# A norm, squares and additions redistributed over GpSimd, TensorE and ScalarE in a fused convolution, adaLN and expert kernel

## The chip, the cores and the metric

One core of one Trainium2 chip runs the whole program. A time is the device time of one execution in microseconds (us), the smaller the better. A run more than 1.5% above the fastest of its kernel counts as slow and is left out of the ratios. A ratio is the mean time of one kernel's fast runs over that of the kernel before's fast runs in the same rounds on the same chip, so it isn't quite the ratio of the medians that stand beside it.

## The reference, cut to what matters

```python
x = A_q                                        # 2048 tokens x 640 channels
sa, ca, ga, sb, cb, gb = (silu(c) @ w_mod)     # six rows of 640
h = layernorm(x) * (1 + ca) + sa               # the first norm
kv = shift_conv(A_k) * A_v                     # 4 taps
y  = irfft(rfft(pad(kv)) * rfft(pad(ssm_k)))[:2048] + kv * ssm_D
x  = x + ga * (h * y)                          # h is needed only here
h2 = layernorm(x) * (1 + cb) + sb              # the second norm
r  = h2 @ w_r ; idx = top8(r)
x  = x + gb * (h2 + scatter(idx, sigmoid(r[idx]) * expert(h2[idx])))
```

The kernel does the long convolution as Fourier transforms by matmul, for five blocks of 128 channels one after the other: transform, a complex product on VectorE, inverse transform, a round trip of the output U through DRAM, a last small transform, and `x += h * y`. After block 4 come the second norm, the choice of the eight tokens, and the expert.

## The kernel before: the parts that the argument touches

The order of the whole program is a list of tokens; each advances one generator by a step. `H` makes h in four groups of four token rows, three steps to a group; `P` is the complex product; `BT` the inverse transform; `AT` the last transform and the update of xq; `GB`, new in the changed kernel, the two gate products. The other tokens are other stages.

```python
def t_H():
    h = h_["h"] = big.tile([P, M, D], BF, name="h", tag="h")
    for m4 in range(4):
        for m in range(4 * m4, 4 * m4 + 4):
            V.tensor_scalar(out=h[:, m, :], in0=xq[:, m, :], scalar1=rs1[:, m:m + 1], scalar2=nm1[:, m:m + 1], ...)
        hq = h[:, 4 * m4:4 * m4 + 4, :]
        yield
        V.tensor_tensor(out=hq, in0=hq, in1=og[:, None, :].to_broadcast([P, 4, D]), op=ALU.mult)
        yield
        V.tensor_tensor(out=hq, in0=hq, in1=sg[:, None, :].to_broadcast([P, 4, D]), op=ALU.add)
        yield

def t_P(b):
    for hk in range(2):
        # ... cut
        V.tensor_tensor(out=T2[:], in0=X, in1=Hi, op=ALU.mult)          # 128 x 2048
        V.tensor_tensor(out=X, in0=X, in1=Hr, op=ALU.mult)
        yield
        V.tensor_tensor(out=Xr, in0=Xr, in1=T2[:, :, 1, :], op=ALU.subtract)   # 128 x 1024
        V.tensor_tensor(out=Xi, in0=Xi, in1=T2[:, :, 0, :], op=ALU.add)
        yield
```

The squares for the second norm are 23 ScalarE activations with an accumulator and nine statistics instructions on VectorE; the root of the first norm is a chain of small VectorE instructions. In the order, all of `H` stands between blocks 2 and 3, ahead of block 2's last store of U.

Of the kernel before, what the change touches and what calls it, by code (L numbers as in the profile page):

```python
# [35 lines left out]
LK0 START TC RA DIAG0 RA TAB0 RAT LG0 LK1 C0:2 TAB0 G0 LG1 TAB1:2 G0*:2 LX G0* DIAG1 C1:2 DIAG2 BG0 LXA0 BG0*  # L36
IT* Sx RAT G1 BG0 G1:3 DIAG3 Sx:2 IT*:2 X0 X0* BG1 LXA1 X0 X0* BG1 LX:2 LW BG1:2 LK2 Sx:4 X1 BX0 BX0*:2 BX0
P0:2 X1:3 BG0 LG2 LW LK3 C2:2 MOD Sx DIAG4 Sx LX LW Sx:2 P0:2 G2:3 BT0 BX1 LXA2 C3 G2 BX1 BT0 Sx:2 BT0 BX1 MOD
LW MOD LW P1 BX1 X2:3 Sx:4 LG3 C3 X2 BT0 MOD LW LXA3 P1:2 LK4 BG2:2 BX2 LG4 P1 BX2:3 BG2:2 MOD:2 OG BT1 P2:4
G3 X3:2 BT1 COL G3:2 H:3 G3 G4:2 C4 BT1 H BT1 H X3:2 C4 LXA4 LU0 G4:2 BG3 BX3:2 H:3 BT2 H:4 BX3 BG3:3 BT2:3 P3  # L40
AT0 P3 LU1 X4:4 AT0 BX3 BG4 P3:2 BX4:3 BG4 AT1 WG BT3 LU2 BT3:3 BG4:2 P4:2 AT1 BX4 R0 BT4:2 P4:2 R0 AT2:2
BT4:2 LU3 AT3 R1 AT3 R1 R2* BS*:2 R2 R3* LU4 AT4:2 BS* S:3 R3 R4* SV R4 S SA:2 WD BS:3 T BS:2 BL N:5 N* T N*
WG N* N:2 T N N* N:3 N* F T F:3 BL F T:2 F:3 T:4
# [17 lines left out]
def _kernel_body(ctx, tc, A_q, A_k, A_v, A_shift_k, A_ssm_k, A_ssm_D,  # L61
# [5 lines left out]

    def dump(name, ap):
        if name in DBG:
            nc.sync.dma_start(out=DBG[name], in_=ap)  # L70
# [6 lines left out]
    psum = ctx.enter_context(tc.tile_pool(name="psum", bufs=4, space=bass.MemoryType.PSUM))  # L77

    def ps_tile(shape, dtype=F32):
        return psum.tile(list(shape), dtype, name="ps", tag="ps")  # L80
# [42 lines left out]
    bias = const.tile([P, 4], F32, name="bias")  # L123
# [25 lines left out]
    cinfo = const.tile([P, 3], BF, name="cinfo")  # L149
    bcol = const.tile([NB * NSEL, 1], F32, name="bcol")  # L150
    gb40 = const.tile([NB * NSEL, P], BF, name="gb40")
# [8 lines left out]
    def t_START():  # L160
# [4 lines left out]
        G = nc.gpsimd  # L165
        for i, v in enumerate((PI, -PI, -math.pi / 2, -4096.0)):
            G.memset(bias[:, i:i + 1], v)
        nc.scalar.activation(out=junk1[:], in_=bias[:, 2:3], func=ACT.Sin)
        iota(pint[:], [[0, 1]], cm=1)
        iota(a4.rearrange("p (a e) -> p a e", e=8), [[4, M], [0, 8]], base=1)  # L170
        iota(pidx[:], [[0, 1]], cm=1)
        make_identity(nc, ident[:])
        iota(erow[:], [[0, M], [1, 8]])
# [4 lines left out]
        for hf in range(2):  # L178
            iota(trig[:, hf, :].rearrange("p (a b) -> p a b", a=8), [[4, 8], [64, P]], base=32 * hf + 1)
            if hf == 0:  # L180
                G.memset(Dt[:], 0.0)
        iota(arow[:], [[1, M], [0, 8]])
        iota(irow[:], [[1, P]])
        G.memset(onesb[:], 1.0)
# [4 lines left out]
        V.tensor_scalar(out=mint[:], in0=pint[:], scalar1=15, scalar2=None, op0=ALU.bitwise_and)  # L189
        V.tensor_copy(out=mcol[:], in_=mint[:])  # L190
        yield

    def t_TC():
# [9 lines left out]
        G.tensor_scalar(out=bcol[:], in0=bcol[:], scalar1=-MAGIC, scalar2=None, op0=ALU.add)  # L203
        G.tensor_scalar(out=cinfo[:, 0:1], in0=mC[:], scalar1=128.0, scalar2=None, op0=ALU.mult)
# [60 lines left out]
    As, HXs, Uds, uAs, diags = {}, {}, {}, {}, {}  # L265
# [21 lines left out]
    def t_C(b):  # L287
        kT, vT = kTs[b], vTs[b]
        kvT = ring.tile([P, S_TOK], BF, name="kvT", tag="V")
        for i2 in range(2):  # L290
            ps = ps_tile([P, 2, 512])
            for i in range(2):
                n0 = 16 + 512 * (2 * i2 + i)
                for j in range(4):
                    nc.tensor.matmul(ps[:, i, :], lhsT=diags[b][:, j, :], rhs=kT[:, n0 - j:n0 - j + 512],  # L295
                                     start=(j == 0), stop=(j == 3))
            V.tensor_tensor(out=kvT[:, 1024 * i2:1024 * i2 + 1024], in0=ps[:].rearrange("p a b -> p (a b)"),  # L297
                            in1=vT[:, 1024 * i2:1024 * i2 + 1024], op=ALU.mult)
            if i2 == 0:
                kvds[b] = dram.tile([P, S_TOK], BF, name="kvd%d" % b)  # L300
            nc.sync.dma_start(out=kvds[b][:, 1024 * i2:1024 * i2 + 1024], in_=kvT[:, 1024 * i2:1024 * i2 + 1024])
            yield
# [20 lines left out]
    T2 = ring.tile([P, 8, 2, P], BF, name="T2", tag="T2")  # L323

    def t_P(b):
        hx = HXs[b]
        for hk in range(2):
# [3 lines left out]
            Hr, Hi = (hx[:, ks, i:i + 1, 0, :].to_broadcast([P, 8, 2, P]) for i in range(2))  # L331
            V.tensor_tensor(out=T2[:], in0=X, in1=Hi, op=ALU.mult)
            V.tensor_tensor(out=X, in0=X, in1=Hr, op=ALU.mult)  # L333
            yield
            V.tensor_tensor(out=Xr, in0=Xr, in1=T2[:, :, 1, :], op=ALU.subtract)
            V.tensor_tensor(out=Xi, in0=Xi, in1=T2[:, :, 0, :], op=ALU.add)
            yield

    def t_BT(b):
        hx = HXs[b]  # L340
        Ud = Uds[b] = dram.tile([P, M, 256], BF, name="Ud%d" % b)
        for hk in range(2):
            U = ring.tile([P, 8, 256], BF, name="U", tag="K", bufs=5)
            for kk in range(2):
# [8 lines left out]
                if kk == 1:  # L353
                    nc.gpsimd.dma_start(out=Ud[:, 8 * hk:8 * hk + 8, :], in_=U[:])  # L354
# [15 lines left out]
    ssq = small.tile([P, 2, M], F32, name="ssq")  # L370
    wcol = const.tile([P, NB, 3], BF, name="wcol")
# [3 lines left out]
    def t_AT(b):  # L375
        h = h_["h"]
        c0 = b * P
        for hb in range(2):
            uA = uAs[b][hb]
            ps = ps_tile([P, 2, M, 32])  # L380
            for bb in range(8):
                o = ps[:, bb // 4, :, (bb % 4) * 8:(bb % 4) * 8 + 8]
                for cs in range(2):
# [3 lines left out]
            t = ring.tile([P, M, 64], BF, name="t", tag="K", bufs=5)  # L387
            cc = slice(c0 + hb * 64, c0 + hb * 64 + 64)
            V.tensor_tensor(out=t[:].rearrange("p m (g j) -> p m g j", g=2), in0=ps[:].rearrange("p g m j -> p m g j"),  # L389
                            in1=h[:, :, cc].rearrange("p m (g j) -> p m g j", g=2), op=ALU.mult)  # L390
            V.tensor_tensor(out=xq[:, :, cc], in0=xq[:, :, cc], in1=t[:], op=ALU.add)  # L391
            yield

    def junk():
        if "junk" not in h_:
            h_["junk"] = ring.tile([P, S_TOK], BF, name="junk", tag="V")
        return h_["junk"]

    def squares(b0, nb, ms):

        dst = ssq[:, 0 if b0 == 0 else 1, :]
        n = nb * P
        for m in ms:
            nc.scalar.activation(out=junk()[:, 0:n], in_=xq[:, m, b0 * P:b0 * P + n], func=ACT.Square,  # L404
                                 accum_out=dst[:, m:m + 1])

    def t_S():
        for q in range(4):
            squares(0, 4, range(4 * q, 4 * q + 4))
            yield  # L410

    def t_SV():
        st = small.tile([P, 9, 2, 3], F32, name="st4")
        sq = small.tile([P, 9, 2], F32, name="sq4")
        for i in range(9):
            V.bn_stats(out=st[:, i].rearrange("p e s -> p (e s)"), in_=xq[:, 7 + i, 512:640])
        V.tensor_tensor(out=sq[:], in0=st[:, :, :, 1], in1=st[:, :, :, 1], op=ALU.mult)
        V.scalar_tensor_tensor(out=sq[:], in0=sq[:], scalar=64.0, in1=st[:, :, :, 2], op0=ALU.mult, op1=ALU.add)
        V.tensor_tensor(out=ssq[:, 1, 7:16], in0=sq[:, :, 0], in1=sq[:, :, 1], op=ALU.add)
        yield  # L420

    def t_SA():
        for ms in (range(0, 3), range(3, 7)):
            squares(4, 1, ms)
            yield

    def t_BS():

        for j in range(8):
            if j % 4 == 0:  # L430
                h_["base", j // 4] = big.tile([P, 8, D], BF, name="base", tag="HX", bufs=2)
            ps = ps_tile([P, 2, 512])
            for i in range(2):
                nc.tensor.matmul(ps[:, i, :], lhsT=ident[:], rhs=gbs[:, 0:512], start=True, stop=False)
                nc.tensor.matmul(ps[:, i, :], lhsT=ident[:], rhs=xq[:, 2 * j + i, 0:512], start=False, stop=True)
            evac(h_["base", j // 4][:, 2 * j % 8:2 * j % 8 + 2, 0:512], ps[:])
            yield

    def t_BL():

        for j in range(2):
            ps = ps_tile([P, 2, 4, P])
            for i in range(2):
                m = 8 * j + 4 * i
                nc.tensor.matmul(ps[:, i], lhsT=ident[:], rhs=gbs[:, None, 512:640].to_broadcast([P, 4, P]),
                                 start=True, stop=False)
                nc.tensor.matmul(ps[:, i], lhsT=ident[:], rhs=xq[:, m:m + 4, 512:640], start=False, stop=True)
            evac(h_["base", j][:, :, 512:640].rearrange("p (i m) d -> p i m d", i=2), ps[:])
            yield

    def t_R(b):
# [3 lines left out]
        xT = ring.tile([P, M, P], BF, name="xT", tag="K", bufs=5)  # L455
        evac(xT[:], pt[:])
        yield
        pr = ps_tile([P, M, 3])
        for m in range(M):
            nc.tensor.matmul(pr[:, m, :], lhsT=xT[:, m, :], rhs=wcol[:, b, :], start=True, stop=True)  # L460
        if b == 0:
            V.tensor_copy(out=rsum[:], in_=pr[:, :, :])
        else:
            V.tensor_tensor(out=rsum[:], in0=rsum[:], in1=pr[:, :, :], op=ALU.add)
        yield
# [34 lines left out]

    def t_COL():
# [8 lines left out]
        V.tensor_tensor(out=gbo, in0=modv[:, 4, :], in1=modv[:, 5, :], op=ALU.mult)  # L510
        V.tensor_tensor(out=gbs, in0=gbs, in1=modv[:, 5, :], op=ALU.mult)
# [6 lines left out]
        nc.gpsimd.memset(wcol[:, :, 2], 1.0)  # L518
# [5 lines left out]
        onesf = early[:, 9728:9984].bitcast(F32)  # L524
        nc.gpsimd.memset(onesf, 1.0)
        pr = ps_tile([P, 2, 512])
        nc.tensor.matmul(pr[:, 0, 0:2], lhsT=onesf, rhs=red[:], start=True, stop=True)
# [26 lines left out]
    def rsqrt(dst, vv, name):  # L554

        n = vv.shape[-1]
        yi = small.tile([P, n], I32, name=name + "i")
# [295 lines left out]
```

## Time and profile before

| | before |
|---|---|
| time, median of 3 runs | 184.8 us |
| VectorE, TensorE, ScalarE, GpSimd busy | 86%, 78%, 74%, 18% |
| last issue of block 2's U store (the "milestone") | 107.6 us (107.58; the prediction has 107.5) |
| last update of xq ends | 147.0 us |
| end of the span | 183.9 us |

A busy share is an average over stages. The three points in time cut the span into a front, a middle and a tail, and each stage is then read by itself. The lines are in the prediction.

### The profile page before, as it was taken

Reading aid. Unit: us, or ns where it says so; the run is one execution under the profiler, and the core shown is the slowest. Engines: PE = TensorE matmul, PEld = TensorE weight load, DVE = VectorE, ACT = ScalarE, POOL = GpSimd, SP = SyncE. Lnnn points to the kernel's source line nnn. Section 1 sums busy time; section 2 is a strip of 40 time slices with the busy share of each in tenths; the row PEclk is TensorE's granted clock in tenths of the full one; section 3 lists DMA queues with packets and bytes.
Section 4 is the critical chain, followed back from the end, with each engine's and each line's share of the span. In section 5 each row is a group of like instructions: output and inputs, shape, how many; then the busy total and the mean of one; then the engine's idle time right before and its main releaser. Section 6 shows DMA issues by size and latency. Waiting matters only on the chain.

```text
span 183.9 us, 4109 instructions
## 1 busy us (share of the span) xinstructions
PE 144.0 (78%) x1664; PEld 112.5 (61%) x1664; DVE 157.7 (86%) x283; ACT 136.2 (74%) x180; POOL 33.2 (18%) x81
## 2 busy tenths in 40 slices
PE   0669989985989999939999969999679578165850
PEld 0225979952768679837679759998577342024840
DVE  5869998988979899977599999989979996999930
ACT  4368789792897979775599979999448999996000
POOL 7997500005001022010010020020200102100003
PEclk9999999999999999995799999999999999955555
DMA  6999989999999999992041999994768099705540
GB/s 108 152 204 278 313 186 326 272 198 274 265 292 320 338 304 309 176 200 114 0 171 61 212 320 324 368 338 183 200 261 224 8 293 362 310 4 219 207 153 2
DMA packets 68668, 40.68 MB, mean 221 GB/s; under 512 B 44904, under 2 KB 64808, under 8 KB 68648
## 3 DMA queue, kind: packets, MB, share of 16 engines
q1 hardware_dynamic: 65160, 35.15, 72.7%
q0 software_dynamic: 1520, 5.25, 7.7%
q10 hardware_dynamic: 1968, 0.01, 0.7%
q8 instruction: 13, 0.21, 0.5%
q14 instruction: 7, 0.06, 0.1%
HBM read 24.67 MB, written 10.50 MB: 191 GB/s over the span
## 4 chain that ended last, share of the span: by engine, by line
DVE 27%; DMA 27%; PE 24%; ACT 12%; issue 6%; SPq 2%; POOLq 1%; POOL 0%; DVEq 0%; ACTq 0%
DMA kT<-in_A_k_dram 9%; PE ps L295 8%; ACT junk L404 7%; DMA kvd<-kvT 7%; DMA uA<-Ud 6%; DVE kvT L297 4%; DVE st L581 4%; PE ps L274 3%; PE ps L314 3%; DVE xq L641 3%; DMA Ud<-U 3%; DVE xq L643 3%; PE ps L384 2%; ACT U L58 2%; ACT A L58 2%
## 5 line engine op out<-in xcount | busy, mean ns | idle before, releaser
L58 ACT CAST A<-ps 128x1024 bf16<-128x1024 f32 x35 | 33.6, 1030 | 8.5 <-PE ps L274 8.5
L58 ACT CAST HX<-ps 128x1024 bf16<-128x1024 f32 x37 | 35.9, 1054 | 2.8 <-PE ps L318 2.8
L314 PE MATMUL ps<-A,FT 128*128 128x256 bf16 x160 | 36.2, 272 | 0.4 <-DVE kvT L297 0.4
L318 PE MATMUL ps<-A,FT 128*128 128x128 bf16 x160 | 35.0, 219 | 0.0
L316 PE MATMUL ps<-A,FT 128*128 128x128 bf16 x160 | 35.0, 219 | 0.0
L295 PE MATMUL ps<-kT,dg 128*128 128x512 bf16 x80 | 21.6, 426 | 7.0 <-DMA kT<-in_A_k_dram 7.0
L58 ACT CAST U<-ps 128x1024 bf16<-128x1024 f32 x20 | 19.8, 1048 | 5.0 <-PE ps L350 2.3
L295 PEld LDWEIGHTS <-dg 128*128 128x128 bf16 x80 | 8.5, 108 | 17.4 <-issue 3.8
L354 POOL DMA_DIRECT2D Ud<-U x10 | 5.7, 572 | 72.9 <-ACT U L58 62.9
L348 PE MATMUL ps<-IT,HX 128*128 128x256 bf16 x80 | 18.1, 273 | 0.8 <-DVE kvT L297 0.8
L350 PE MATMUL ps<-IT,HX 128*128 128x256 bf16 x80 | 18.1, 273 | 0.0
L297 DVE TENSOR_TENSOR kvT<-ps,vT 128x1024 bf16<-128x1024 f32 x10 | 12.1, 1220 | 6.9 <-PE ps L295 5.7
L318 PEld LDWEIGHTS <-FT 128*128 128x128 bf16 x160 | 15.7, 98 | 1.8
L316 PEld LDWEIGHTS <-FT 128*128 128x128 bf16 x160 | 15.6, 98 | 0.9 <-issue 0.8
L314 PEld LDWEIGHTS <-FT 128*128 128x128 bf16 x160 | 15.7, 98 | 0.3
L237 POOL TENSOR_SCALAR dg<-ident,shk_f 128x128 bf16<-128x128 bf16 x16 | 10.3, 659 | 20.0 <-PE ps L295 20.0
L384 PE MATMUL ps<-RAT,uA 128*128 128x128 bf16 x160 | 10.4, 219 | 4.2 <-DMA uA<-Ud 4.2
L404 ACT ACTIVATE junk<-xq 128x512 bf16<-128x512 bf16 (+1 forms) x23 | 12.2, 533 | 2.0 <-DVE xq L391 1.3
L389 DVE TENSOR_TENSOR t<-ps,h 128x1024 bf16<-128x1024 f32 x10 | 12.2, 1218 | 1.7 <-PE ps L384 1.6
L581 DVE BATCH_NORM_STATS2 st<-xq 128x6 f32<-128x320 bf16 x32 | 13.2, 478 | 0.5 <-DMA xq<-in_A_q_dram 0.5
L274 PE MATMUL ps<-RA,gA 128*128 128x256 bf16 x80 | 12.3, 309 | 1.5 <-DVE gA L281 1.5
L333 DVE TENSOR_TENSOR HX<-HX 128x2048 bf16<-128x2048 bf16 x10 | 12.2, 1225 | 0.4
(218 smaller groups left out, 308.6 us busy)
## 6 DMA issues: line engine op xcount, KB each, us to landing
Ud<-U POOLq DMA_DIRECT2D x10, 512.0 KB, 6.0
uA<-Ud SPq DMA_DIRECT2D x10, 512.0 KB, 6.5
early<-in_w_mod_dram SPq DMA_DIRECT2D x6, 800.0 KB, 7.3
gA<-in_A_ssm_k_dram SPq DMA_DIRECT2D x5, 512.0 KB, 5.0
kvd<-kvT SPq DMA_DIRECT2D x10, 256.0 KB, 3.9
xq<-in_A_q_dram SPq DMA_DIRECT2D x4, 640.0 KB, 6.4
xA<-kvd SPq DMA_DIRECT2D x5, 512.0 KB, 4.8
out_dram<-xq SPq DMA_DIRECT2D x4, 640.0 KB, 3.1
```

The lines of the kernel that those rows point to most:

```text
L58: self.nc.scalar.copy(out=out, in_=in_)
L274: nc.tensor.matmul(ps[:, bb // 2, :, (bb % 2) * 8:(bb % 2) * 8 + 8], lhsT=src[:, 4 * g4 + bb, :], rhs=RA[:].rearrange("p k c e -> p (k c) ...
L295: nc.tensor.matmul(ps[:, i, :], lhsT=diags[b][:, j, :], rhs=kT[:, n0 - j:n0 - j + 512], start=(j == 0), stop=(j == 3))
L297: V.tensor_tensor(out=kvT[:, 1024 * i2:1024 * i2 + 1024], in0=ps[:].rearrange("p a b -> p (a b)"), in1=vT[:, 1024 * i2:1024 * i2 + 1024], ...
L314: nc.tensor.matmul(ps[:, i], lhsT=FT[:, 0, k2, :], rhs=A[:, 2 * k2:2 * k2 + 2, u, :], start=True, stop=False)
L316: nc.tensor.matmul(ps[:, i, 0, :], lhsT=FT[:, 1, k2, :], rhs=A[:, 2 * k2 + 1, u, :], start=False, stop=False)
L318: nc.tensor.matmul(ps[:, i, 1, :], lhsT=FT[:, 2, k2, :], rhs=A[:, 2 * k2, u, :], start=False, stop=True)
L348: nc.tensor.matmul(ps[:, i, :], lhsT=hx[:, k2, 0, 1, :], rhs=IT[:, k2, 1:3, :].rearrange("p a b -> p (a b)"), start=True, stop=False)
L350: nc.tensor.matmul(ps[:, i, :], lhsT=hx[:, k2, 1, 1, :], rhs=IT[:, k2, 0:2, :].rearrange("p a b -> p (a b)"), start=False, stop=True)
L384: nc.tensor.matmul(o, lhsT=uA[:, bb, cs * P:(cs + 1) * P], rhs=RAT[:, cs, :].rearrange("p (m e) -> p m e", e=8), start=(cs == 0), stop=(cs ...
L404: nc.scalar.activation(out=junk()[:, 0:n], in_=xq[:, m, b0 * P:b0 * P + n], func=ACT.Square, accum_out=dst[:, m:m + 1])
L581: V.bn_stats(out=st1[:, m, hf, :], in_=xq[:, m, hf * 320:hf * 320 + 320])
```

## The change

Its intent is to unload VectorE and ScalarE: squares become diagonal blocks of Gram matrices on TensorE, part of the elementwise work goes to GpSimd, the eviction of PSUM is divided anew between ScalarE and VectorE, warm-up matmuls raise TensorE's clock, and the expert's input is gathered from raw x. A star in the order now also means "the other engine": `off()` gives GpSimd for a starred token.

```diff
+    def off():
+        return nc.gpsimd if evac.vector else V
 ...
 def t_H():
-                V.tensor_scalar(out=h[:, m, :], in0=xq[:, m, :], scalar1=rs1[:, m:m + 1], ...
+                off().tensor_scalar(out=h[:, m, :], in0=xq[:, m, :], scalar1=rs1[:, m:m + 1], ...
 ...
 def t_P(b):
-            V.tensor_tensor(out=Xr, in0=Xr, in1=T2[:, :, 1, :], op=ALU.subtract)
+            off().tensor_tensor(out=Xr, in0=Xr, in1=T2[:, :, 1, :], op=ALU.subtract)
 ...
 def t_GB():
+        off().tensor_tensor(out=gbo, in0=modv[:, 4, :], in1=modv[:, 5, :], op=ALU.mult)
+        off().tensor_tensor(out=gbs, in0=gbs, in1=modv[:, 5, :], op=ALU.mult)
 ...
-        rsqrt(rs1[:], var1, "n1")
+        nc.gpsimd.tensor_tensor(out=rs1[:], in0=var1[:], in1=bias[:, 4:5].to_broadcast([P, M]), op=ALU.pow)
 ...
+    def t_WU():                       # 13 zero matmuls at the start
+    def t_GR():                       # 64 matmuls of 32 columns a block: squares
 ...
 ORDER (tail of the part between blocks 2 and 4)
-... OG ... H:3 G3 ... H BT1 H ... LU0 G4:2 BG3 BX3:2 H:3 BT2 H:4 BX3 BG3:3 BT2:3 P3 ...
+... BT2:2 P3 COL BT2 LU0 BG4:2 X4:2 H* H:2 X4:2
+BG4:2 BX4:4 H* H:2 H* WG H:2 H* H WG:2 H P4 LU2 AT0* BT3:3 ... AA1 GB* BT4:2
```

Two things happen to h: its 16 scale-and-shift instructions change engine, and all of h moves behind block 2's last store.

## The prediction

> **What bounds the kernel now.** I read the engine shares first, then the chain that ended last, then the timeline in windows. The page's first part says that no engine is a wall by itself:
>
> ```profile
> span 183.9 us, 4109 instructions
> PE 144.0 (78%) x1664; PEld 112.5 (61%) x1664; DVE 157.7 (86%) x283; ACT 136.2 (74%) x180; POOL 33.2 (18%) x81
> PEclk9999999999999999995799999999999999955555
> DMA  6999989999999999992041999994768099705540
> ```
>
> VectorE (DVE) is busiest; GpSimd (POOL) is nearly free; the 16 DMA engines are full until about 85 us (tens of the row "DMA"); the granted TensorE clock halves in the tail. Summing the windows, VectorE works about 94 us of the first 107.5, ScalarE 82 and TensorE 92. The end of that stretch is the last issue of block 2's U store (block = 128 of the 640 channels); I use it as a milestone. The chain has three pieces after it: the round trip of the last convolution output through DRAM, ScalarE's squares, and the VectorE tail.
>
> ```profile
> 122.40 5.91 DMA Ud<-U
> 128.38 4.69 DMA uA<-Ud
> ...
> 137.61 0.70 DVE xq L391
> 138.33 0.73 ACT junk L404 x2
> ...
> 152.99 0.41 ACT junk L404 x2
> 153.43 0.19 DVE tot L653
> ...
> 174.42 0.68 issue
> 175.21 3.58 DMA out_dram<-xq
> ```
>
> The columns are start, length, and what. The last update of xq ends at 147.03 (timeline, L391 at 146.34). From there: squares done 153.4 (+6.4), normalisation coefficients done 156.7 (+9.6), last addition of the output 175.2 (+28.2), end 183.9 (+36.9). So a time is "milestone, plus 39.5 us to the last xq update, plus 36.9 us", and 0.9 more to the measured 184.8.
>
> **What the Trainium skill says.** (1) "GPSIMD Engine Reference", section 4.1 Engine selection: GpSimd is about half as fast as VectorE with two inputs, and "1-input is roughly line-rate". The trace has only narrow ones:
>
> ```profile
> 10.03 0.32 POOL L205 TENSOR_SCALAR MC<-irow,mC 128x16 bf16<-128x16 f32 x1
> ...
> 10.95 0.61 POOL L207 TENSOR_SCALAR tri<-irow,pidx 128x128 bf16<-128x128 f32 x1
> ...
> 68.68 1.24 POOL L281 TENSOR_TENSOR gA<-gA,Dt 128x16 bf16<-128x16 bf16 x1 [2.16 <-DMA gA<-in_A_ssm_k_dram]
> ```
>
> and VectorE's timeline beside it:
>
> ```profile
> 67.31 1.23 DVE L332 TENSOR_TENSOR T<-HX 128x2048 bf16<-128x2048 bf16 x1
> 68.57 1.22 DVE L333 TENSOR_TENSOR HX<-HX 128x2048 bf16<-128x2048 bf16 x1
> ```
>
> From 16 to 128 columns costs 0.29 us, 2.6 ns a column, which doesn't look like line rate. (2) "SBUF — State Buffer", section Who interferes with whom: a VectorE instruction with two SBUF inputs and a GpSimd one that reads SBUF exclude each other, and the later blocks fully. The trace agrees: that gA addition started under L333, which ended at 69.79, and lasted 1.24 us where its sister at 20.54 took 0.27. (3) "TensorE: Matmul & The Clock Gate", Part 1: TensorE runs at half clock until it has been busy about 3.4 us. The trace agrees: the first 16 convolution matmuls took 5.97 us (373 ns each), a later eight 1.74 (218 ns). (4) "TensorEngine Tiling (Array Packing)", sections Instruction Overhead and Restrictions: some 60 cycles a matmul whatever its width, and column tiles lose the fast weight load. No run here shows it yet; narrow 8-column matmuls took 2.00 us for 70, 28.6 ns a pair of load and matmul.
>
> **The change part by part.** The "ring" of four two-bank PSUM tiles is the same four buffers as before until the router's transposes; then one is split into two one-bank tiles and three remain. No gain or loss is expected from it by itself: four tiles were there all along.
>
> Start. Thirteen zero matmuls warm the clock, and the filter block goes before the convolution. Worth at most 16 x (373 - 218) = 2.5 us; I take -2.
>
> VectorE up to the last U store. Removed: 8 of the 20 subtractions and additions of the complex product, 8 x 0.69 = 5.5; the 16 scale-and-shift of the first norm (L592), 6.0; its ten-instruction square root, 10 x 0.21 = 2.1 (one power on GpSimd instead); four kvT products and three t products that ScalarE evicts first, 7 x (1.22 - 0.69) = 3.7. Added: 18 evictions of A, HX and IT in place of 11, 7 x 1.21 = 8.5. Net -8.8. ScalarE: -6 A, -3 HX, +2 IT, +4 kvT, +3 t: -6.2 - 3.2 + 3.7 + 4.1 + 3.1 = +1.5. Up to the milestone I count about 86 us on VectorE and 91 on ScalarE in the new order, against 94 and 82: VectorE's surplus is gone, and ScalarE becomes the fuller. With ten or twelve microseconds of waits around 91 the milestone comes at 102 instead of 107.5: -5.5, of which the -2 of the start is a part; so -3.5 besides it.
>
> The first norm on GpSimd. The order puts all 16 [128 x 640] scale-and-shift instructions on GpSimd behind block 2's last U store, and VectorE's queue has the eight [128 x 2560] products and additions of h (1.49 each) directly in front of the complex product of block 4. Before, all of h was done at 106.4, ahead of the milestone. Now ScalarE has 12 evictions there (12.6 us) in which it hides. At line rate one takes about 0.28 + 640 x 1.04 ns = 0.95 us (estimate from the skill's remark), 15 for all, and a part excludes VectorE's 12 us; at the trace's slope it takes 0.28 + 640 x 2.6 ns = 1.9 us (estimate), 31 for all, 40 with the lock. The last four also wait for the buffer of the up weights. After h come 8.3 us of complex product, the last inverse transform, and the round trip through DRAM. I charge +3 in the good case and +20 in the bad one. I weigh the good case about twice as heavily, because so finely interleaved an order would hardly put all sixteen there had they cost 40 us; that is a guess about the author, not a reading.
>
> GpSimd's eight 1024-column additions: about 1024 x 2.2 ns = 2.3 us each (estimate from section 3.1's 4497 ns at 2048), beside VectorE's work, but colliding: +1.
>
> Round trip. Block 4's two U stores go on SyncE's queue: before, issue and start took 0.53 + 1.28 us on GpSimd. -1.
>
> Tail. Squares: 16 x 0.63 + 7 x 0.31 + 23 x 0.19 = 16.6 us leave ScalarE. In their place 320 matmuls, 64 a block, at least 64 x 28.6 ns = 1.8 us a block; two blocks and a base tile stand between the last transposes and the sum, so 1.2 + 1.8 + 0.9 + 1.8 = 5.7 us, then a masked product and a reduction of 512 columns, 0.7 each by VectorE's rate, and the shorter root: coefficients again at about +9.6 to +10.5. ScalarE then does 16 normalisations (11 before) at 0.82 and four casts: 17 us, to +27; VectorE has 16 output instructions of 0.82 = 13.1 and 4.4 of router work from +11: +29. Before it was +28.2. The gather reads raw xq and no longer waits for ScalarE, so the expert input is ready some 4 us sooner, but its next product (hT) stands behind all output instructions in VectorE's order: hidden. The last store is half the size, -1. Down weights on ScalarE's queue: transfers that were hidden anyway. Tail: 0.
>
> Sum, good case: 184.8 - 2 - 3.5 + 3 + 1 - 1 + 0 = 182.3. The whole kernel has 8.8 us less on its busiest engine, and I have given it only 5.5; the waits at 40 to 45 and 80 to 90 us (VectorE 3.8, 3.1 and 3.4 of 5 there) may go as well, 4 more: 178. I take 180 as the centre.
>
> **The rivals.** First: GpSimd becomes the bound of the first norm. For it: the slope and the lock above, and that VectorE has nothing else in its queue meanwhile. Against it: the skill's line-rate remark, and the order itself. It would make 198 to 202. Second: the gain is larger, because ScalarE's relief from squares and VectorE's from 8.8 us both turn into time. For it: VectorE is 86% busy, over 96% in many windows. Against it: the tail is bound by VectorE's output instructions after +11. It would make 170 to 174. Third: DMA bounds the front, being full until 85 us with the same bytes; then the front gives nothing: 184 to 186.
>
> **Range and chances.** The good case and the second rival give 170 to 182, the first 198 to 202. The middle 8 of 10 go from 169 to 200. Faster by over 2% (below 181.1) 0.52, within 2% (to 188.5) 0.19, slower 0.29.
>
> **What would show it.** Right: [128 x 640] scale-and-shift on GpSimd at about 1 us, VectorE's idle time before L663 under 5 us, the milestone at 100 to 104, the first convolution matmuls at 218 ns, the last xq update at 140 to 145, the tail 36 to 38 us after it. Wrong: these instructions at 1.7 to 2 us, L663 waiting 20 us for GpSimd, ScalarE and TensorE idle around 115 to 140 us, the clock halved there. If the 64 Gram matmuls of a block take over 3 us, the tail is longer by twice the excess.

## The result, and the profile after

The changed kernel takes 197.53 us (median of 4 runs, 195.5 to 198.88) against 185.75 (4 runs). The ratio of the fast runs is 1.070 (95% interval 1.050 to 1.090): slower. The profiled run is the longest of the four, but its clock (0.870) lies within that of the other three (0.868 to 0.879), and its main reading, a product of 11.93 us, recurs in the profile of e2_gb (11.88).

The page's first two parts, after; columns as in the prediction:

```profile
span 197.1 us, 4727 instructions
PE 148.9 (76%) x1983; PEld 117.7 (60%) x1983; DVE 156.6 (79%) x242; ACT 131.2 (67%) x141; POOL 71.2 (36%) x113
PEclk9979999999999999999999995555899889955555
DMA  7996999999999999989997699000289004912540
```

GpSimd's work has doubled, the work of the others is about the same, and the span is 13 us longer. The clock's row has a stretch of fives ahead of the tail's, at slices 25 to 28 (118 to 138 us), and the row "DMA" falls to 0 at 26 to 28: something stood still there. The waits of TensorE and VectorE in the whole span that concern it (engine, line, who ended the wait; us in total, times, longest):

```profile
PE p L421 <- DVE HX L408: 19.4, 1, 19.4
DVE h L663 <- POOL h L659: 6.2, 1, 6.2
```

TensorE waits 19.4 us in one piece for block 4's complex product on VectorE. So what does VectorE do? The timeline, GpSimd (POOL) and VectorE together (start, length, what, and in brackets the idle time before it with what ended it):

```profile
100.26 0.54 POOL L427 DMA_DIRECT2D Ud<-U  x1 [1.23 <-ACT U L59]
100.85 10.32 POOL L659 TENSOR_SCALAR h<-xq,rs,nm 128x640 bf16<-128x640 bf16 x12
104.33 11.93 DVE L663 TENSOR_TENSOR h<-h,modv 128x2560 bf16<-128x2560 bf16 x1 [6.22 <-POOL h L659]
111.12 0.35 POOL L673 MEMSET wu<- 128x320 bf16 x1
111.47 3.44 POOL L659 TENSOR_SCALAR h<-xq,rs,nm 128x640 bf16<-128x640 bf16 x4
116.29 4.21 DVE L665 TENSOR_TENSOR h<-h,modv 128x2560 bf16<-128x2560 bf16 x1
116.39 1.41 POOL L581 TENSOR_TENSOR modv<-modv 128x640 bf16<-128x640 bf16 x1
117.75 1.40 POOL L582 TENSOR_TENSOR modv<-modv 128x640 bf16<-128x640 bf16 x1
120.43 1.48 DVE L663 TENSOR_TENSOR h<-h,modv 128x2560 bf16<-128x2560 bf16 x1
121.94 1.49 DVE L665 TENSOR_TENSOR h<-h,modv 128x2560 bf16<-128x2560 bf16 x1
```

GpSimd runs at 0.86 us an instruction, twelve without a gap, a memset, and four more. VectorE's first product starts when its four rows are there (104.33) and takes 11.93 us, where the later ones take 1.48. It ends 1.35 us after GpSimd's last scale-and-shift (114.91). The first addition takes 4.21 and ends 1.35 us after GpSimd's second gate product. That time is booked as busy: VectorE's share of 79% holds 13 us in which it worked on nothing. In the groups (busy time, mean ns of one, idle before), after and then before:

```profile
L663 DVE TENSOR_TENSOR h<-h,modv 128x2560 bf16<-128x2560 bf16 x4 | 16.4, 4093 | 6.2 <-POOL h L659 6.2
L659 POOL TENSOR_SCALAR h<-xq,rs,nm 128x640 bf16<-128x640 bf16 x16 | 13.8, 869 | 0.0
```

```profile
L596 DVE TENSOR_TENSOR h<-h,modv 128x2560 bf16<-128x2560 bf16 x4 | 6.0, 1493 | 0.1
L592 DVE TENSOR_SCALAR h<-xq,rs,nm 128x640 bf16<-128x640 bf16 x16 | 6.0, 438 | 0.0
```

The mean of the same product went from 1493 to 4093 ns with no change of shape: that is the reading that points to a lock (each engine shuts the other out for a time), which the experiments then test.

| | before | after |
|---|---|---|
| milestone (last U store of block 2) | 107.6 | 100.3 |
| h complete | 106.4 | 129.3 |
| product of block 4 complete | 129.3 | 137.3 |
| last update of xq ends | 147.0 | 161.1 |
| end of the span | 183.9 | 197.1 |

The front gained 7.3 us, the tail is 36.0 us against 36.9, and the middle went from 39.5 to 60.9 us. From GpSimd's first scale-and-shift (100.85) to the end of the last addition of h (129.3) are 28.4 us, and the sum of both engines' own work there is 13.8 (GpSimd, h) + 11.9 (VectorE, eight of 1.49) + 2.8 (GpSimd, gates) = 28.5. Next to nothing was done at the same time. Of this, VectorE had to wait 3.5 us for its first four rows in any case.

### The profile page after: what moved, and what is told of

The parts are those of the page before. It is cut to its first block, busy times and chain, and to the rows that moved or that the text cites.

```text
span 197.1 us, 4727 instructions
## 1 busy us (share of the span) xinstructions
PE 148.9 (76%) x1983; PEld 117.7 (60%) x1983; DVE 156.6 (79%) x242; ACT 131.2 (67%) x141; POOL 71.2 (36%) x113
## 3 DMA queue, kind: packets, MB, share of 16 engines
q0 software_dynamic: 1232, 4.21, 5.4%
## 4 chain that ended last, share of the span: by engine, by line
PE 49%; DVE 28%; ACT 7%; POOL 5%; DMA 4%; issue 3%; ACTq 1%; POOLq 1%; DVEq 0%; SPq 0%
DVE h L663 8%; PE ps L366 6%; PE ps L345 6%; PE ps L385 6%; DVE h L665 4%; PE ps L456 4%; PE ps L564 4%; PE ps L389 3%; PE ps L387 3%; DMA uA<-Ud 3%; ACT base L59 2%; PE p L423 2%; PE ps L421 2%; PE p L345 2%; PE ps L423 2%
## 5 line engine op out<-in xcount | busy, mean ns | idle before, releaser
L59 ACT CAST HX<-ps 128x1024 bf16<-128x1024 f32 x28 | 28.0, 1071 | 2.3 <-PE ps L389 2.3
L389 PE MATMUL ps<-A,FT 128*128 128x128 bf16 x128 | 28.0, 219 | 0.0
L387 PE MATMUL ps<-A,FT 128*128 128x128 bf16 x128 | 28.0, 219 | 0.0
L421 PE MATMUL p<-IT,HX 128*128 128x256 bf16 x36 | 9.1, 288 | 19.4 <-DVE HX L408 19.4
L59 ACT CAST U<-p 128x1024 bf16<-128x1024 f32 x9 | 9.6, 1065 | 20.0 <-issue 19.8
L663 DVE TENSOR_TENSOR h<-h,modv 128x2560 bf16<-128x2560 bf16 x4 | 16.4, 4093 | 6.2 <-POOL h L659 6.2
L421 PEld LDWEIGHTS <-HX 128*128 128x128 bf16 x80 | 8.2, 102 | 20.9 <-DVE HX L408 19.7
L59 ACT CAST A<-ps 128x1024 bf16<-128x1024 f32 x20 | 19.9, 1046 | 0.8 <-PE ps L345 0.8
L659 POOL TENSOR_SCALAR h<-xq,rs,nm 128x640 bf16<-128x640 bf16 x16 | 13.8, 869 | 0.0
L57 DVE CAST A<-ps 128x1024 bf16<-128x1024 f32 x9 | 11.0, 1222 | 3.1 <-PE ps L345 3.0
L405 DVE TENSOR_TENSOR T<-HX 128x2048 bf16<-128x2048 bf16 x10 | 12.8, 1284 | 0.1
```

The source lines that it names most:

```text
L59: self.nc.scalar.copy(out=out, in_=in_)
L387: nc.tensor.matmul(ps[:, i, 0, :], lhsT=FT[:, 1, k2, :], rhs=A[:, 2 * k2 + 1, u, :], start=False, stop=False)
L389: nc.tensor.matmul(ps[:, i, 1, :], lhsT=FT[:, 2, k2, :], rhs=A[:, 2 * k2, u, :], start=False, stop=True)
L421: nc.tensor.matmul(ps[:, i, :], lhsT=hx[:, k2, 0, 1, :], rhs=IT[:, k2, 1:3, :].rearrange("p a b -> p (a b)"), start=True, stop=False)
L659: off().tensor_scalar(out=h[:, m, :], in0=xq[:, m, :], scalar1=rs1[:, m:m + 1], scalar2=nm1[:, m:m + 1], op0=ALU.mult, op1=ALU.add)
```

## The experiments

Theory: GpSimd's instructions and VectorE's two-input products of h exclude each other, so their times add on the path to block 4's product. Rivals: GpSimd is merely late and slow (no exclusion); or the loss sits in another part of the change. Every kernel below agreed with the reference in the comparison.

| run | edit | median us (runs) | ratio to before (95%) |
|---|---|---|---|
| changed kernel | | 197.5 (4) | 1.070 (1.050 to 1.090) |
| e1_vector | h on VectorE | 187.1 (20) | 1.006 (1.002 to 1.010) |
| e2_gb | gates on VectorE | 194.5 (4) | 1.045 (1.035 to 1.055) |
| e3_both | both, "the repaired kernel" | 183.6 (4) | 0.985 (0.972 to 0.998) |
| e6_reduce | one-input VectorE work, wrong values | 188.1 (4) | 1.014 (1.002 to 1.026) |
| e5_half | half of h on VectorE | 188.9 (4) | 1.016 (1.003 to 1.028) |
| e7_before | the kernel before, h on GpSimd | 192.5 (4) | 2 fast runs only |
| e8_p | repaired, additions on VectorE | 186.5 (20) | 1.007 (1.002 to 1.011) |
| e9_root | repaired, root on VectorE | 185.2 (22) | 0.994 (0.989 to 0.999) |
| e11_nowarm | repaired, no warm-up | 185.9 (22) | 1.004 (1.000 to 1.008) |
| e10_order | repaired, block 4's product earlier | 183.9 (4) | 0.988 (0.976 to 1.001) |
| e12_mixed | e10 and more on ScalarE | 182.0 (6) | 0.983 (0.974 to 0.991) |
| e13_plain | e12 with one output on VectorE again | 181.0 (6) | 0.973 (0.967 to 0.979) |

### e1_vector: h back on VectorE

```diff
-... LU0 BG4:2 X4:2 H* H:2 X4:2 BG4:2 BX4:4 H* H:2 H* WG H:2 H* H WG:2 H P4 ...
+... LU0 BG4:2 X4:2 H H:2 X4:2 BG4:2 BX4:4 H H:2 H WG H:2 H H WG:2 H P4 ...
```

> Changed kernel, with the 16 scale-and-shift instructions of h back on VectorE. Theory (lock: GpSimd's instructions and VectorE's two-input products of h exclude each other, so their times add): VectorE starts h at about 98 instead of 104.3 and needs 16 x 0.38 + 8 x 1.49 = 18 us, so h ends at 116 instead of 129.2; the two gate products still on GpSimd take 2.8 back, the clock that no longer halves gives some 3: 184 to 187 us. Rival 1 (GpSimd is just slower and late, no lock): the same direction, but the gain is only the 6.2 us wait of the first product and the 3.5 us of the last group: 187 to 191. Rival 2 (the loss sits in other parts: power on GpSimd, additions on GpSimd, three PSUM tiles): over 192.

Median 187.1, mean of the 14 fast runs 186.5, inside the theory's range: 10 us of the loss (means of the fast runs, 196.9 and 186.5) came from 16 instructions on GpSimd that VectorE does in 6.0. h ended at 117.1 here, with VectorE's part starting at 99.1; the gate products, still on GpSimd, now stretched one instruction of block 4's product (2.23 us instead of 1.23) and a product of the xq update (1.88 instead of 0.68). Rival 2 falls. Rival 1 overlaps the theory's range at its edge, so this run alone doesn't rule it out.

### e2_gb: only the gate products back

```diff
-... AA1 GB* BT4:2
+... AA1 GB BT4:2
```

> Changed kernel, with only the two gate products (128x640, 1.4 us each on GpSimd) back on VectorE. Theory (lock): the first addition of h, 4.21 us in the changed kernel, drops to 1.5; two products of 0.48 are added later: h ends 2.7 us sooner, the total is 194.5 to 196. Rival (no lock; the 4.21 us were a wait for something else): 197 to 198.5, addition still near 4.2.

Median 194.5. VectorE's first addition took 1.49 us instead of 4.21, its first product still 11.88:

```profile
105.61 11.88 DVE L663 TENSOR_TENSOR h<-h,modv 128x2560 bf16<-128x2560 bf16 x1 [6.20 <-POOL h L659]
117.52 1.49 DVE L665 TENSOR_TENSOR h<-h,modv 128x2560 bf16<-128x2560 bf16 x1
```

So two GpSimd instructions of 1.4 us, which nobody waits for, cost 2 to 3 us (3.0 by the medians, 2.1 by the means of the fast runs, 196.9 and 194.8). Between e1 and e3 the same edit is worth 3.0 us (means of the fast runs, 186.5 and 183.5).

### e3_both: the repaired kernel

```diff
- H* ... GB*
+ H ... GB          (both edits above)
```

> Both of the two edits: no GpSimd work beside h any more. Theory (lock): h ends at about 116, nothing is lost behind it, complex product of block 4 ends at about 124.5, last update of xq 20 us later, tail 36: 180 to 184 us, near or a little under the kernel before. Rival 2 (other parts lose the time): over 190.

Median 183.6, within the theory's range; the interval of the ratio ends just under 1. VectorE's timeline at the first and last instruction of h, and TensorE's longest wait:

```profile
98.24 1.50 DVE L659 TENSOR_SCALAR h<-xq,rs,nm 128x640 bf16<-128x640 bf16 x4
...
114.74 1.49 DVE L665 TENSOR_TENSOR h<-h,modv 128x2560 bf16<-128x2560 bf16 x1
```

```profile
PE p L421 <- DVE HX L408: 6.2, 1, 6.2
```

h is complete at 116.2, 13 us before the changed kernel's, and the spans differ by 14.3. So the loss is explained. What isn't yet: the milestone is at 100.5, 7 us before that of the kernel before, and the tail is one us shorter, but the whole gains only some 2 us (means of the fast runs, 185.4 and 183.5). The middle still takes 46.4 us instead of 39.5. e10 to e13 look into that.

### e6_reduce: VectorE work that doesn't need the second input

```diff
-            V.tensor_tensor(out=hq, in0=hq, in1=og[:, None, :]..., op=ALU.mult)
-            yield
-            off().tensor_tensor(out=hq, in0=hq, in1=sg[:, None, :]..., op=ALU.add)
+            V.tensor_reduce(out=red4[:], in_=hq, axis=mybir.AxisListType.X, op=ALU.add)   # result unused
+            yield
```

> Changed kernel with all GpSimd work left as it is, but the product and the addition of each group of h replaced on VectorE by one reduction of the same 128x2560 with a single SBUF input (wrong values on purpose: h lacks the modulation). It costs about 2.7 us a group[...], 10.7 in all against 11.9. Theory (lock needs two SBUF inputs): the reductions run beside GpSimd, none is longer than 3 us, the last ends 2.7 us after GpSimd's last scale-and-shift (about 117.7 against 129.2): total 182 to 187. Rival 1 (waiting for GpSimd, not the lock): the first VectorE instruction is again stretched to about 10 us, and only 1.2 us is gained: 195 to 197.

GpSimd's work and place are those of the changed kernel. The timeline:

```profile
101.33 10.32 POOL L659 TENSOR_SCALAR h<-xq,rs,nm 128x640 bf16<-128x640 bf16 x12
104.81 2.82 DVE L664 TENSOR_REDUCE red<-h 128x4 f32<-128x2560 bf16 x1 [6.22 <-POOL h L659]
108.25 2.82 DVE L664 TENSOR_REDUCE red<-h 128x4 f32<-128x2560 bf16 x1 [0.61 <-POOL h L659]
...
115.42 2.82 DVE L664 TENSOR_REDUCE red<-h 128x4 f32<-128x2560 bf16 x1 [0.92 <-POOL h L659]
118.16 2.56 DVE L405 TENSOR_TENSOR T<-HX 128x2048 bf16<-128x2048 bf16 x1
```

All four reductions take 2.82 us beside GpSimd; none is stretched, and each starts as soon as its group is there. The next two-input instruction is stretched again (2.56 against 1.22, beside the gate products). This decides between theory and rival 1: with the same wait for GpSimd, h ends at 118.2 instead of 129.3, because the VectorE instruction is one that GpSimd doesn't hold up. A reduction differs from a product in its operation and in what it writes (4 columns, not 2560) as well as in having one SBUF input, so this run alone doesn't show that the number of inputs decides; e5 below has a VectorE instruction with one SBUF input that was held up. The Trainium skill's "SBUF — State Buffer", section Who interferes with whom, says the same of both forms: a reduction never contends, and two SBUF inputs do against a GpSimd read. The total, 188.1, is a us above the expected range. The comparison with the reference passed although h lacks its modulation, so on these inputs it doesn't notice this.

### e5_half: half a dose

```diff
-... X4:2 H* H:2 X4:2 BG4:2 BX4:4 H* H:2 H* WG H:2 H* H WG:2 H P4
+... X4:2 H H:2 X4:2 BG4:2 BX4:4 H* H:2 H WG H:2 H* H WG:2 H P4
```

> Changed kernel, with the scale-and-shift of the first and third group of h on VectorE and of the second and fourth still on GpSimd. Theory (times add): 8 x 1.49 + 8 x 0.38 + 8 x 0.86 = 21.9 us from 98.2, h ends at 120 (116 with none on GpSimd, 126.5 with all when the gate products are taken out); the gate products on GpSimd add up to 2.8: 188 to 191 us. Rival (no addition, GpSimd hidden beside VectorE's own groups): h ends at 115, total 183 to 186.

h ended at 120.1 and the median is 188.9: the sum of the two engines' times gave both, within about 1 us (the last addition, 2.56 us, holds 1.1 that belong to the gate products). But the exclusion looks different:

```profile
L659 POOL TENSOR_SCALAR h<-xq,rs,nm 128x640 bf16<-128x640 bf16 x8 | 10.8, 1360 | 0.0
L665 DVE TENSOR_TENSOR h<-h,modv 128x2560 bf16<-128x2560 bf16 x4 | 8.2, 2040 | 0.1
```

```profile
98.35 1.50 DVE L659 TENSOR_SCALAR h<-xq,rs,nm 128x640 bf16<-128x640 bf16 x4
108.91 2.20 DVE L659 TENSOR_SCALAR h<-xq,rs,nm 128x640 bf16<-128x640 bf16 x4
```

Here GpSimd's mean rises from 869 to 1360 ns and that of VectorE's additions to 2040: they take turns, and each waits for one instruction of the other. In the changed kernel GpSimd isn't stretched at all and VectorE waits for twelve. In both the engines' times add. The two lower lines, from VectorE's timeline, show something else: its own scale-and-shift, which reads one tile and the two scalars of each row, takes 1.50 us for four without GpSimd beside it and 2.20 where GpSimd starts during the last two. In the trace the fourth took 1.00 us instead of 0.43, beside a scale-and-shift on GpSimd, and the third 0.57, beside its memset. So products with two SBUF inputs aren't the only VectorE instructions that GpSimd holds up.

### e7_before: the same move alone, in the kernel before

```diff
-                V.tensor_scalar(out=h[:, m, :], in0=xq[:, m, :], ...
+                nc.gpsimd.tensor_scalar(out=h[:, m, :], in0=xq[:, m, :], ...
```

> The kernel before, with nothing changed but the 16 scale-and-shift instructions of h moved to GpSimd. Theory (the two engines' times add): VectorE loses 16 x 0.38 = 6.0 us of work and is shut out for up to 16 x 0.86 = 13.8 us, so +7.8 in a stretch that VectorE bounds, less where it would have waited anyway: ratio to before 1.01 to 1.05. Rival (GpSimd runs beside VectorE): ratio 0.97 to 1.00.

Four runs, 190.6 to 194.3; two count as fast, mean 191.0 against 185.2 for the kernel before, a ratio of 1.03 without an interval. The direction is the theory's. Both kinds of exclusion occur in this one trace; the longest:

```profile
97.66 6.89 POOL L592 TENSOR_SCALAR h<-xq,rs,nm 128x640 bf16<-128x640 bf16 x8
99.41 6.48 DVE L598 TENSOR_TENSOR h<-h,modv 128x2560 bf16<-128x2560 bf16 x1
```

Eight GpSimd instructions in a row, 0.86 each and not stretched, and the addition of 1.49 us waits them out. So the move is bad in the old order too, by about 6 us as far as two fast runs can tell.

### e8_p: the additions of the complex product

```diff
- P0* ... P0* ... P1* ... P2*        (repaired kernel)
+ P0  ... P0  ... P1  ... P2
```

> The repaired kernel (h and the gate products on VectorE), with the eight subtractions and additions of the complex product that the change gave to GpSimd also back on VectorE. VectorE gets 8 x 0.68 = 5.5 us more, GpSimd loses 8 x 2.1 = 17. If these additions lie beside work that does not need the shared port, the repaired kernel is right to have them on GpSimd: 184.5 to 187 here. If they block VectorE as h did: 181 to 183 here, faster than the repaired kernel (183.6).

Mean of the fast runs 186.5, against 183.5 of the repaired kernel: these eight are better on GpSimd, by some 3 us. The milestone moves from 100.5 (100.3 to 102.5 in the nine profiles with the same front) to 103.3. The changed kernel's timeline shows why the same engine helps here:

```profile
61.99 2.12 POOL L408 TENSOR_TENSOR HX<-HX,T 128x1024 bf16<-128x1024 bf16 x1
62.26 1.23 DVE L57 CAST A<-ps 128x1024 bf16<-128x1024 f32 x1
```

GpSimd needs 2.12 us where VectorE needs 0.68, but beside it VectorE has an eviction from PSUM, which has no SBUF input and isn't stretched. Beside all eight VectorE has mostly evictions (1.2 us), products with one input from PSUM (1.22) or statistics instructions (0.48), none of them longer than elsewhere. One addition, at 75.12, began under a product with two SBUF inputs; it took 2.44 us itself, and the product its usual 1.23.

### e9_root: the root of the first norm

```diff
-        nc.gpsimd.tensor_tensor(out=rs1[:], in0=var1[:], in1=bias[:, 4:5]..., op=ALU.pow)
+        rsqrt(rs1[:], var1, "n1")
```

> The repaired kernel, with the first norm's power on GpSimd (2.94 us, VectorE waits 3.1 for it) replaced by the old chain of small VectorE instructions (about eleven of 0.2 us, 2.3 us). If VectorE's time up to the milestone is what counts, this gains 0.8 us: ratio to the repaired kernel 0.995. If something else sets the milestone there, nothing: 1.00. If the power on GpSimd had cost more than its wait (a port held, a late load), the gain is 2 us or more.

Ratio 0.994 (0.989 to 0.999), that of the repaired kernel 0.985 (0.972 to 0.998): the intervals overlap, so a gain of 0.8 us isn't seen, and a gain of 2 us or more is unlikely. The power costs 2.94 us on GpSimd for 16 columns, and VectorE waits 3.1 for it; the chain took 2.2 in this run.

### e11_nowarm: without the warm-up

```diff
-WU LG0 SA SC RA SG ...
+LG0 SA SC RA SG ...
```

> The repaired kernel without the 13 warm-up matmuls. By the prediction's step for the start, the first 16 convolution matmuls go from 3.9 us back to about 6 and everything behind them is 2 us later: 185.5 us against 183.6. Rival (the front is bound by transfers, the earlier start is absorbed before the milestone): no difference.

Mean of the fast runs 186.0, 1.8 us above e9_root's of the same rounds (which differs from it by the root too) and 2.5 above the repaired kernel's four runs of another batch. So the warm-up is worth 1 to 2.5 us. The milestone in its profile is 101.8 against 100.5. That isn't clear of noise: in the nine profiles whose front is the same (the changed kernel, e1, e2, e3, e5, e6, e10, e12 and e13) it lies between 100.3 and 102.5. And the first 16 convolution matmuls took 4.64 us here, not 6. In the eleven profiles with the warm-up they take 3.6 to 4.8, so their gain over the 6.0 us of the kernel before isn't the warm-up's. The filter block now ahead of them is the likely cause; no run tested it.

### e10_order, e12_mixed, e13_plain: where the rest of the gain is

```diff
 e10 (against the repaired kernel)
-BG4:2 BX4:4 H H:2 H WG H:2 H H WG:2 H P4 LU2 AT0* BT3:3 WG:2 BT3 P4:3 BT4:2 AA0 AT0 AA0 AT1* AA1 GB BT4:2
+BG4:2 BX4:4 H H:2 P4 WG P4 WG:2 P4 LU2 P4 BT3:3 WG:2 BT3 BT4:4 H H:2 H H:2 AT0* AA0 AT0 AA0 AT1* AA1 GB
 e12 (against e10)
-... BT3 BT4:4 H H:2 H H:2 AT0* AA0 AT0 AA0 AT1* AA1 GB AT1 ... AT2
+... BT3 H BT4:4 H:2 H H:2 AT0* AA0 AT0* AA0 AT1* AA1 GB AT1* ... AT2*
+ rows 8 to 15 of h: nc.scalar.activation(out=h[:, m, :], in_=xq[:, m, :], func=Identity, scale=rs1, bias=nm1)
 e13 (against e12)
-AT0* AA0 AT0*
+AT0 AA0 AT0*
```

> The repaired kernel, with the complex product and inverse transform of block 4 ahead of the last two groups of h in VectorE's order. In the repaired kernel TensorE waits 6.2 us for that product, restarts at half clock, and the round trip of block 4 begins only at 129. Theory: the product ends at about 115.4 instead of 124.1, TensorE's wait falls to 1 to 3 us, the clock stays full, h ends at 124 inside the round trip; the last update of xq comes at 140 to 143 instead of 146.9: 177 to 180 us. Rival (VectorE's total bounds, whatever the order): 183 to 184.

183.9, no faster than the repaired kernel's 183.6. The product of block 4 was complete at 119.0 instead of 124.2, and TensorE's wait for it fell from 6.2 to 1.3 us, as the theory had it; but the last update of xq ended at 147.1, against 146.9. VectorE began h 2.0 us later in this profile (100.3; 98.2 to 99.7 elsewhere, with the same instructions before it), so from there to that update it took 46.8 us instead of 48.7: some gain, far from the 4 to 7 us expected. VectorE was busy without a break from 111.4 to 140.5, and the half clock came back at 128 to 136, when TensorE waited 6.1 us for VectorE's updates of xq. So the rival is nearly right: from the start of h to that update VectorE was busy for 43.1 of the 46.8 us. The times of e3 and e10 can't tell a gain of 2 us from none, as their intervals show.

> The re-ordered kernel (block 4's product ahead of the last two groups of h), with the last eight scale-and-shift instructions on ScalarE, which is half idle between 116 and 145, and three more of the inverse convolution's outputs evicted by ScalarE before VectorE's product. Theory (VectorE's sum of work from 98 to 147 is now the bound, ScalarE takes work without shutting VectorE out): 8 x 0.38 = 3.0 and 3 x 0.53 = 1.6 us less on VectorE: last update of xq at 142 to 143.5, 179 to 180.5 us. Rival (the round trip of block 4 or ScalarE's order becomes the bound): 183 to 185.

182.0, about 2 us less than e10, not 4. From the start of h to the last update of xq it took 46.2 us. The first output of block 0 kept VectorE waiting 1.54 us for ScalarE's copy, which stood behind ScalarE's new work. Part of the gain went into a new wait, as the rival had it: in that stretch VectorE's busy time fell from e10's 43.1 us to 38.9, and the stretch only by 0.6. By the intervals e12 isn't set apart from e10.

> The mixed kernel, with only the first output of the inverse convolution of block 0 read by VectorE straight from PSUM again. There ScalarE's queue (eight scale-and-shift, four evictions) kept VectorE waiting 1.5 us for its copy. Theory (VectorE's line from 98 to 147 is the bound): the wait of 1.5 goes, 0.53 comes back as work: 1 us less, 181 us. Rival (TensorE at half clock and its wait of 3.4 us for a PSUM tile set the pace there): no difference, 182.

181.0. VectorE's timeline after h:

```profile
124.24 1.49 DVE L669 TENSOR_TENSOR h<-h,modv 128x2560 bf16<-128x2560 bf16 x1
125.82 1.23 DVE L79 TENSOR_TENSOR t<-ps,h 128x1024 bf16<-128x1024 f32 x1
```

The wait is gone: the output is read straight from PSUM 0.1 us after h, and the middle, from the start of h, is down to 45.0 us. The ratio to the kernel before is 0.973 (0.967 to 0.979), faster by 2.7%, so this version beats both. Whether e13 beats e12 isn't settled; the intervals of e3, e10, e12 and e13 overlap from one to the next.

## Why the prediction was right or wrong

The time lay inside the range (169 to 200), near its upper end, and 17 us above the centre. The range held only because it reached up towards the first rival; what was thought likeliest, faster (0.52), didn't come, and slower had 0.29. By its steps:

- **Start, -2.** Right in size: e11 puts the warm-up at 1 to 2.5. The first 16 convolution matmuls took 4.1 us in the changed kernel instead of 6.0 (256 ns each, not the 218 of the sign), but that isn't the warm-up's doing (e11: 4.64 without it).
- **The milestone, 102.** Right in the number (100.3 here, up to 102.5 in other profiles with the same front), not in its working. ScalarE was to be the fuller there, with 91 us and some eleven of waits. Up to the milestone the trace has ScalarE at 83.0 us (83.0 before), VectorE at 81.1 (forecast 86; 93.8 before) and TensorE at 94.0 (90.4 before). The fullest engine is TensorE, which the step didn't weigh, so that it came within 2 us is in part luck. The eight additions on GpSimd, charged +1 for collisions, collided with nothing where it mattered; with VectorE's relief they are worth 3 us (e8), where VectorE's work is shown to matter.
- **The first norm on GpSimd, +3 in the good case.** This is the step that failed. Its duration was right: 0.95 us estimated, 0.87 measured, so the line-rate remark held and the slope taken from narrow instructions was misleading. The failure is in "Now ScalarE has 12 evictions there (12.6 us) in which it hides" and "a part excludes VectorE's 12 us". What mattered wasn't ScalarE's time but VectorE's, and not a part but all of it is excluded: 13.8 + 11.9 us add up. Against the repaired kernel, h on GpSimd costs 11 us (e2 against e3), where +3 was charged.
- **Left out altogether.** The two gate products on GpSimd, 2 to 3 us (e2; e1 against e3). No step named them, as nothing waits for their result.
- **The first rival, 198 to 202.** It came nearly true in its size (197.5), and only half in its cause: it stood on instructions of 1.9 us plus the lock. The instructions were at line rate; the lock made up the rest, with the gates. Its signs came: VectorE held up before and in L663, ScalarE and TensorE idle from 116 to 133, the clock at half there. The sign "L663 waiting 20 us" came as 6.2 us of wait and 10.4 us booked as work.
- **The middle, otherwise 39.5.** Wrong by 7 us even without GpSimd (e3: 46.4). "Before, all of h was done at 106.4, ahead of the milestone" was seen, but the 18 us of VectorE's work on h that moved behind the milestone were treated as hidden; the sum for the front took out the scale-and-shift and never the 11.9 us of products. Part of what the front gained was this work, moved. Most of block 3's product moved the other way, so that in e3 VectorE is busy for 40.9 us of the middle against 37.0 before, and idle for 5.5 against 2.5. e10 points to VectorE as the bound of that stretch: a better order alone gave 1.9 us there and nothing that shows in the time. e12 and e13 took about 4 us of work from VectorE, and the stretch fell by 0.6 and 1.8 us, so other engines are then close behind.
- **Round trip, -1.** Not seen: from the end of block 4's product to the last update of xq it took 17.7 us before, 23.8 in the changed kernel and 22.7 in e3. No run isolates why. The prediction's lines for it, at 122.40 and 128.38, are block 3's; block 4's stores were issued at 129.37 and 132.84.
- **The other rivals.** The second (170 to 174) didn't come, as the tail kept its length. The third (transfers bound the front, nothing gained there) didn't either: with the same 40.7 MB the front is 7.3 us shorter.
- **Tail, 0.** Right in the sum: 36.0 against 36.9. The first normalisation starts 8.0 us after the last update of xq instead of 9.7, sooner than forecast, but the last addition ends at +28.1 as before (+28.2). The Gram matmuls were cheaper than the least estimate, 0.66 us for 64 against 1.8:

```profile
134.34 0.66 PE L477 MATMUL pg<-xT 128*32 128x32 bf16 x64
```

(timeline of the repaired kernel). It didn't shorten the tail, which has as many output instructions on VectorE as before (16) and now 16 normalisations on ScalarE (11 before).
- **Two small readings.** From 0 to 107.5 us ScalarE is busy for 83.0 and TensorE for 90.4 us, not 82 and 92. And the profiled execution of the kernel before took 185.71 us, so the span lacks 1.8 us of it, not 0.9. Neither changes the argument.

What stays open: why GpSimd held VectorE out for a whole run of instructions in the changed kernel and took turns with it in e5. In the traces it took turns where VectorE was in a row of two-input instructions as GpSimd's began, and it held VectorE out where VectorE came to a run already under way; the addition at 116.29, which began 0.1 us ahead of the gate products, doesn't fit that cleanly, nor does the product at 88.45 in e7, which met a GpSimd run under way and took 1.51 us, unstretched. No run varied this by itself. VectorE's stretched scale-and-shift in e5 wasn't varied either.

## What to carry to other kernels

Work given to GpSimd was free here beside evictions from PSUM, statistics and reductions on VectorE (e8, e6). Beside products with two SBUF inputs it was added to VectorE's time at GpSimd's slower rate, even if nobody waited for its result, and VectorE's own scale-and-shift from SBUF to SBUF was held up too (e5). So look at what VectorE does beside it, form by form. Look for the mean of an unchanged instruction that has grown: a blocked engine is booked as busy. And when work moves behind a milestone, an earlier milestone is no gain until the sum of the bounding engine's work on both sides of it has been taken.

## What the Trainium skill lacked or had wrong

- "SBUF — State Buffer", Who interferes with whom: it says that whoever issues first holds the pair for the whole instruction, and that the other blocks. It doesn't say what happens in a row of GpSimd instructions. Here the waiting VectorE product got no turn in the gaps of a run (11.93 us in the changed kernel, 6.48 in e7), while in e5 the two took turns (additions of 2.04 us on average instead of 1.49).
- "GPSIMD Engine Reference", section 4.1: the remark that one-input work is roughly at line rate held (0.87 us for 640 columns), but VectorE did the same bf16 instruction in 0.38, so "line rate" isn't parity. The page names the contention with two-input work elsewhere (its table of specifications and its key points), but not in this section, where the engine is chosen; here it cost 13 us.
- "TensorEngine Tiling (Array Packing)", Instruction Overhead: some 60 cycles a matmul whatever its width. The section doesn't say how this counts when column tiles work side by side, which the page allows. The 64 matmuls of 32 columns, in four column tiles, took 0.66 us, 10.3 ns each, less than half of the 28.6 ns a pair that the kernel before shows for untiled 8-column matmuls.
- No page that I read gives the cost of a power on GpSimd: 2.94 us for 128 x 16.
